# Delta-rule attention and two MoE layers on one core: the first set's preparation emitted as one block, ahead of the weight conversion

## Chip, cores, metric

The kernel runs on one core of a Trainium2 chip. The metric is the device time of one launch in microseconds (us). All times below that begin with a position ("at 61.2") are counted from the first instruction of the profiled execution.

## What is computed

```python
# attention: a state of 48 x 48 per batch and head, updated token by token
k_n = k / (norm(k) + 1e-6)
for t in range(S):                      # S = 768; 4 batches x 8 heads
    y[t] = q[t] @ state
    state += beta[t] * outer(k_n[t], v[t] - k_n[t] @ state)
x = y reshaped to 3072 x 384
# first layer
h = ((x @ w1) * (x @ w2)) @ w3 @ w_out   # w1, w2: 384x1024, w3: 1024x1024, w_out: 1024x384
# second layer
h = h @ w_in; softmax-weighted, normalised per token, scaled by g_ln
out = ln @ w_out2
```

The six weight matrices arrive as 64-bit floats, everything else as 32-bit floats.

## The kernel before

**Attention in chunks.** The 768 tokens of a batch are cut into chunks of 64; heads go in pairs (NP = 4), and six sets of eight chunks (SETC = 8) follow each other. For a set the kernel needs, of every chunk, the Gram matrix of its normalised keys and the product of keys and queries, then the inverse of a small triangular matrix per chunk and head, then a chain of matmuls that carries the state from chunk to chunk. The prologue does this for set 0 before the main loop starts; later sets are prepared inside the main loop, between the matmuls of the first layer.

**Preparation of two chunks**, of which set 0 has four (i = 0 to 3):
- `norm(i)` (L244): square on ScalarE (ACT) at L249, sum on VectorE (DVE) at L250, square root on ACT at L251, add, reciprocal and product on DVE (L252 to L254), then copies of the keys by DMA (tile `kst`).
- `prep_t(i)` (L267): TensorE (PE) transposes the keys (`pk`, L270) and the queries (`pq`, L275) into PSUM; ACT (L272) and DVE (L277) copy them into the one buffer `KQ`, ACT copies parts of the queries into `QA` (L280, L281).
- `prep_g(i)` (L287): 16 matmuls in two PSUM tiles `pg` (L295); ACT copies the Gram parts (L300 to L303) into `GD`, which is a view of the tile `GT`, and into `G21`; DVE masks the key-query part into `QA` (L306).

`KQ` exists once, so the matmuls of one i must end before the copies of the next i start.

**The inverse** (`invert`, L325) works on all of set 0 at once: DVE transposes `GT` into `D1n` (L326), GpSimd (POOL) zeroes `GT`, and 31 pairs of DVE operations (L336, L342) follow, each waiting for the one before. `invert_end` (L346) transposes the result into `Dt` (L347) and `D1n` (L348). The first matmul of the main loop (`pm`, L374) reads `Dt`.

**Weight conversion** is one generator, `wg`. A block of a matrix is loaded by DMA into one of five staging slots (tiles `stage_a`, twice, and `raw_w2s`, three of them). For each half of a block DVE takes the low words (L140), ACT the high words (L143), DVE shifts (L150) and a custom operation adds (L187). The order of the blocks is: four of `w_out`, eight of `w3`, three of `w1`, three of `w2`. A `w3` block is then transposed by PE (`w3p`, L551), copied by ACT (L553) into one of two areas, and multiplied with `w_out` (`wps`, L558): eight products of 384 columns for each of the eight blocks, which sum up in one PSUM tile that exists once. ACT and DVE split the sum (L226, L227) into `Ws`, the product of both matrices; only then is the PSUM tile free for the next block. A slot is loaded again when its block has been converted and, for `w3`, transposed. One `next(wg)` is one small step of this; `conv(x)` takes x steps.

**What sets the order.** A scheduler in the tile framework places the instructions of each engine when the program is built, from the order in which the code emits them and from costs of its own; each engine then runs its list in order. `held[0]` names an instruction behind which the steps of `conv` are kept (`tc.issue_after`), here the last ACT copy of the preparation just emitted. From L787 on the matmuls' order is fixed by hand, up to the end of the main loop.

The prologue's core (L727 to L747):

```python
norm(1)
for i in range(SETC // 2):
    prep_t(i)
    if 0 < i < SETC // 2 - 1:
        norm(i + 1)
    conv(P0)          # P0 = 4
    prep_g(i)
    conv(2 * P0)
held[0] = None
for z, ins in enumerate(invert(0)):
    conv(0.5, ins)
    ...
```

Of the kernel before, what the change touches and what calls it, by code (L numbers as in the profile page):

```python
# [8 lines left out]
F32 = mybir.dt.float32  # L9
# [3 lines left out]
AF = mybir.ActivationFunctionType  # L13
# [7 lines left out]
def kernel(  # L21
# [15 lines left out]
    nc = tc.nc  # L37
# [25 lines left out]
    P0, C0 = 4, 24  # L63
# [10 lines left out]
    const = ctx.enter_context(tc.tile_pool(name="const", bufs=1))  # L74
# [49 lines left out]
    GD = GT.rearrange("p (u j) -> p u j", j=HC)  # L124
# [119 lines left out]
    def norm(i):  # L244
        kt = kt_of(i).rearrange("t p (e x) -> t p e x", e=2)[:, :, :, 0:D]
        sq = small(NP * 2 * D).rearrange("t (p e d) -> t p e d", e=2, d=D)
        ss = pr.tile([128, NP, 2], F32, name="ss")
        rn = pr.tile([128, NP, 2, 1], F32, name="rn")
        nc.scalar.activation(out=sq, in_=kt, func=AF.Square)  # L249
        nc.vector.tensor_reduce(out=ss, in_=sq, axis=AX.X, op=ALU.add)  # L250
        nc.scalar.activation(out=ss, in_=ss, func=AF.Sqrt)  # L251
        nc.vector.tensor_scalar(out=ss, in0=ss, scalar1=1e-6, scalar2=None, op0=ALU.add)  # L252
        nc.vector.reciprocal(out=rn[:, :, :, 0], in_=ss)
        nc.vector.tensor_tensor(out=kt, in0=kt, in1=rn.to_broadcast([128, NP, 2, D]), op=ALU.mult)  # L254
        for cc in range(2):
            sl = (chunk_of(i) + 2 * cc) % RQ
            for h in range(2):
                o = 64 * (1 - h)
                nc.sync.dma_start(
                    out=kst[sl * 2 // RQ][64 * h:64 * h + 64, sl % (RQ // 2)],  # L260
                    in_=kt_of(i)[64 * cc:64 * cc + 64, :, o:o + D],
                )
# [4 lines left out]
    def prep_t(i):  # L267
        pk = ps_prep.tile([128, NP, 128], F32, tag="prep", name="pk")
        for p in range(NP):
            nc.tensor.transpose(pk[:, p, :], kt_of(i)[:, p, :], ident)  # L270
        r = pk.rearrange("r p (c t) -> r c p t", c=2)
        nc.scalar.copy(out=KQ[0:KA, :, :, 0:C], in_=r[0:KA])  # L272
        pq = ps_prep.tile([128, NP, 128], F32, tag="prep", name="pq")
        for p in range(NP):
            nc.tensor.transpose(pq[:, p, :], qt_of(i)[:, p, :], ident)  # L275
        r = pq.rearrange("r p (c t) -> r c p t", c=2)
        (nc.vector.tensor_copy if i < SETC else nc.scalar.copy)(out=KQ[0:KA, :, :, C:128], in_=r[0:KA])  # L277
        sl = chunk_of(i) % RQ
        qa, sl = qa_of(sl)
        nc.scalar.copy(out=qa[0:64, sl:sl + 3:2, :, 1, :], in_=r[0:64])  # L280
        held[0] = nc.scalar.copy(out=qa[64:KA, sl:sl + 3:2, :, 0, :], in_=r[64:KA])  # L281
        if i < 2:
            load(i + 4)
        if i > 3 and i + 2 < NT128:
            load(i + 2)

    def prep_g(i):  # L287
        for cc in range(2):
            c = chunk_of(i) + 2 * cc
            (qa, sl), u0 = qa_of(c % RQ), c % SETC * NP  # L290
            pg = ps_prep.tile([128, NP, 128], F32, tag="prep", name="pg")
            for p in range(NP):
                for h in range(2):
                    r = slice(64 * (1 - h), 64 * (1 - h) + D)
                    nc.tensor.matmul(  # L295
                        pg[64 * h:64 * h + 64, p, :], KQ[r, cc, p, 0:C], KQ[r, cc, p, :],
                        start=True, stop=True, skip_group_check=True,
                    )
            gd = GD[:, u0:u0 + NP, :]
            nc.scalar.copy(out=gd[:, :, :], in_=pg[:, :, 0:HC])  # L300
            nc.scalar.copy(out=G21[:, c % SETC], in_=pg[:, :, 0:HC])
            nc.scalar.copy(out=gd[32:64], in_=pg[32:64, :, HC:C])
            held[0] = nc.scalar.copy(out=gd[96:128], in_=pg[96:128, :, HC:C])  # L303
            for h in range(2):
                r = slice(64 * h, 64 * h + 64)
                nc.vector.tensor_tensor(  # L306
                    out=qa[r, sl, :, h, :], in0=pg[r, :, C:128],
                    in1=mask[r].unsqueeze(1).to_broadcast([64, NP, C]), op=ALU.mult,
                )
# [3 lines left out]
    def load_beta():  # L313
        for b in range(B):
            nc.sync.dma_start(
                out=bd.rearrange("(o k b) p e g i -> o b (p e) k (g i)", k=CPB, b=2)[b // 2, b % 2],
                in_=beta[b].rearrange("h (k x) -> h k x", k=CPB),
            )
        t = bd.rearrange("(n c) p e g i -> e g (c p) n i", c=SETC)
        for h in range(2):  # L320
            for g in range(2):
                r = 64 * h + 32 * g
                nc.sync.dma_start(out=bl[r:r + 32], in_=t[1 - h, g])
# [345 lines left out]
    def weights_first():  # L669
        a = moe.tile([128, 4096], F32, tag="gh", name="stage_a")  # L670

        def slot(tag):
            return lambda: wts.tile([128, 2 * DFF], F32, tag=tag, name="raw_" + tag)

        a0, a1 = (lambda: a[:, 0:2 * DFF]), (lambda: a[:, 2 * DFF:4 * DFF])
        b = [slot(t) for t in ("w2s0", "w2s1", "w2s2")]
        items = list(weights_w([a0, a1] + b))
        items += weights_ab(w1, w1s, "w1s", [b[0], b[1], b[2]])
        items += weights_ab(w2, w2s, "w2s", [
            a0, a1, lambda: moe.tile([128, 2 * DFF], F32, tag="xb", name="raw_xb", bufs=2),  # L680
        ])
        return convert(items, small, queue, 1)

    make_identity(nc, ident)
    wg = weights_first()
    for i in range(4):
# [8 lines left out]
    for h in range(2):  # L695
        nc.gpsimd.affine_select(
            out=mask[64 * h:64 * h + 64], in_=mask[64 * h:64 * h + 64], pattern=[[1, C]],
# [8 lines left out]
    held = [None]  # L706

    def conv(x, ins=None):
        acc[0] += x
        if acc[0] < 1:  # L710
            return
        with (tc.issue_after(ins.ins) if ins is not None and c_done[0] >= CA else tc.issue_after(held[0].ins) if held[0] is not None else nullcontext()):
            while acc[0] >= 1:
                next(wg, None)
                acc[0] -= 1
# [3 lines left out]
    come = nc.gpsimd.tensor_copy(out=seen, in_=qt_of(2)[:, 0, 64:65])  # L719
    with tc.issue_after(come.ins):  # L720
        next(wg)
    nc.gpsimd.memset(GD, 0.0)
    load_beta()
    for c in range(0, RX, 2):
        load_v(c)
# [2 lines left out]
    for i in range(SETC // 2):  # L728
        prep_t(i)
        if 0 < i < SETC // 2 - 1:  # L730
            norm(i + 1)
        conv(P0)
        prep_g(i)
        conv(2 * P0)

    held[0] = None
    for z, ins in enumerate(invert(0)):
# [281 lines left out]
```

## Time and profile before

| | us |
|---|---|
| median of 3 runs (865.22 to 867.65) | 865.59 |
| span of the profiled execution, first to last instruction | 863.0 |
| PE busy (of the span) | 808.5 (94%) |
| DVE busy | 577.3 (67%) |
| ACT busy | 468.3 (54%) |
| POOL busy | 42.4 (5%) |

For the profiled execution no time besides its span is given; the median of the runs is 2.6 us longer than that span, which is what lies around it. "Busy" is the union of an engine's instructions; PE's weight loads are listed apart (PEld). In a timeline a row gives the start, the time taken, the engine, the line of the code, the operation, what is written from what, the count, and in brackets how long the engine had been idle and what ended that. In a window's row the numbers in brackets are counts, and the last three columns are the granted clock of PE as a share of full speed, the busy share of the DMA engines, and GB/s. The granted clock is shown as 1.00 until the first event that the profile holds, so for the first 40 us it is read from durations.

### The profile page before, as it was taken

The numbers are of one execution on the slowest core, as the hardware profiler recorded it, in microseconds if no ns is written. First come the engines' busy times: TensorE is split into PE (matmuls) and PEld (weight loads), VectorE is DVE, ScalarE is ACT, GpSimd is POOL, SyncE is SP. The second block draws the span as 40 slices with busy tenths as digits, with TensorE's granted clock in tenths as the row PEclk, the third lists the DMA queues.
The fourth block names the chain that finished last, engine by engine and source line by source line (L and its number), as shares of the span: only waits on it lengthen the run. The fifth ranks groups of instructions, "written<-read, shape, count | busy, mean of one in ns | idle before, by whom it ended". The sixth has DMA issues, their size and how long they took to land.

```text
span 863.0 us, 22978 instructions
## 1 busy us (share of the span) xinstructions
PE 808.5 (94%) x9488; PEld 738.5 (86%) x9488; DVE 577.3 (67%) x1426; ACT 468.3 (54%) x1127; POOL 42.4 (5%) x94
## 2 busy tenths in 40 slices
PE   4599678999999999999999999999999999999998
PEld 4365466999889999999999999999989999999997
DVE  3889996985497559755975596457656555555553
ACT  4574578457736773576467744566434443443442
POOL 5010000000000000000000000000001000000000
PEclk9999859999999999999999999999999999999999
DMA  9999814041403331333133113043331221221200
GB/s 226 289 235 163 128 20 83 13 93 35 93 26 63 73 75 35 73 70 68 35 65 68 39 38 94 12 135 109 118 125 57 74 64 55 74 65 55 74 28 28
DMA packets 140569, 70.65 MB, mean 82 GB/s; under 512 B 107056, under 2 KB 130864, under 8 KB 138672
## 3 DMA queue, kind: packets, MB, share of 16 engines
q1 hardware_dynamic: 138688, 57.64, 29.3%
q0 software_dynamic: 1776, 11.54, 4.1%
q8 instruction: 75, 1.23, 0.6%
q14 instruction: 30, 0.25, 0.1%
HBM read 47.91 MB, written 14.25 MB: 72 GB/s over the span
## 4 chain that ended last, share of the span: by engine, by line
PE 45%; issue 23%; DVE 16%; ACT 8%; DMA 6%; POOL 2%; SPq 0%; POOLq 0%; ACTq 0%; DVEq 0%
PE pab L585 17%; PE px L609 6%; PE pg L295 4%; DVE tmp L336 3%; PE wps L558 3%; DVE GT L342 2%; PE pu L445 2%; PE pw L419 2%; PE py L488 2%; DMA stage_i<-in_moe_w_in_dram 2%; PE pst L470 1%; PE pm L398 1%; PE ph L909 1%; POOL vr L939 1%; DMA st_o<-in_moe_w_out_dram 1%
## 5 line engine op out<-in xcount | busy, mean ns | idle before, releaser
L585 PE MATMUL pab<-xb,w1s 128*128 128x256 f32 x864 | 123.6, 288 | 5.1 <-DVE asg L593 4.5
L585 PE MATMUL pab<-xb,w2s 128*128 128x256 f32 x864 | 119.2, 283 | 0.0
L585 PEld LDWEIGHTS pab<-xb,w1s 128*128 128x128 f32 x864 | 109.7, 191 | 9.1 <-DVE asg L593 6.1
L609 PE MATMUL px<-gh,Ws 128*128 128x256 f32 x864 | 112.2, 286 | 0.6 <-ACT gh L594 0.5
L585 PEld LDWEIGHTS pab<-xb,w2s 128*128 128x128 f32 x864 | 110.6, 192 | 0.0
L609 PEld LDWEIGHTS px<-gh,Ws 128*128 128x128 f32 x864 | 105.5, 191 | 2.3 <-ACT gh L594 0.7
L962 PE MATMUL po<-w4s,ln 128*128 128x384 f32 x432 | 79.8, 338 | 0.0
L594 ACT CAST gh<-asg 128x256 fp32r<-128x256 f32 x96 | 38.9, 405 | 72.4 <-DVE asg L593 71.6
L909 PE MATMUL ph<-wis,x 128*128 128x512 f32 x288 | 76.7, 401 | 0.0
L962 PEld LDWEIGHTS po<-w4s,ln 128*128 128x128 f32 x432 | 76.1, 188 | 0.0
L925 ACT ACTIVATE e<-ph,nm 128x1024 f32<-128x1024 f32 x24 | 26.8, 1116 | 87.4 <-DVE nm L924 86.0
L593 DVE TENSOR_TENSOR asg<-pab,asg 128x256 f32<-128x256 f32 x96 | 40.4, 421 | 50.4 <-ACT asg L592 50.2
L342 DVE TENSOR_TENSOR GT<-GT,tmp 128x31 f32<-128x31 f32 (+15 forms) x186 | 63.5, 341 | 4.6
L336 DVE TENSOR_TENSOR tmp<-D1n,GT 128x31 f32<-128x31 f32 (+15 forms) x186 | 62.9, 338 | 3.4 <-ACT GT L328 0.2
L306 DVE TENSOR_TENSOR QA<-pg,mask 64x256 f32<-64x256 f32 x96 | 40.5, 422 | 35.6 <-ACT GT L303 29.1
L295 PE MATMUL pg<-KQ 48*64 48x128 f32 x768 | 54.8, 294 | 8.4 <-DVE KQ L277 7.4
L909 PEld LDWEIGHTS ph<-wis,x 128*128 128x128 f32 x288 | 52.4, 189 | 10.5 <-issue 0.2
L592 ACT COPY asg<-pab 128x256 f32<-128x256 f32 x96 | 35.5, 370 | 44.3 <-PE pab L585 41.0
L295 PEld LDWEIGHTS pg<-KQ 48*64 48x64 f32 x768 | 47.4, 147 | 12.3 <-ACT raw_w2s L143 6.0
L924 DVE TENSOR_REDUCE nm<-ph 128x1 f32<-128x1024 f32 x24 | 29.4, 1224 | 40.4 <-PE ph L909 40.4
L926 DVE SCALAR_TENSOR_TENSOR hs<-ph,e 128x1024 f32<-128x1024 f32 x24 | 29.4, 1225 | 30.9 <-ACT e L925 30.9
L595 DVE TENSOR_TENSOR gh<-asg,gh 128x256 fp32r<-128x256 f32 x96 | 40.5, 422 | 13.9 <-ACT gh L594 13.4
(157 smaller groups left out, 1347.8 us busy)
## 6 DMA issues: line engine op xcount, KB each, us to landing
x2d<-xs SPq DMA_DIRECT2D x36, 256.0 KB, 2.3
x<-x2d SPq DMA_DIRECT2D x24, 384.0 KB, 3.7
X<-in_v_dram SPq DMA_DIRECT2D x48, 96.0 KB, 2.9
out_dram<-ot SPq DMA_DIRECT2D x24, 192.0 KB, 1.9
ktok<-in_k_dram SPq DMA_DIRECT2D x22, 192.0 KB, 3.6
qtok<-in_q_dram SPq DMA_DIRECT2D x22, 192.0 KB, 3.6
kst<-ktok SPq DMA_DIRECT2D x88, 48.0 KB, 3.0
raw_w2s<-in_moe_w_dram POOLq DMA_DIRECT2D x4, 1024.0 KB, 8.9
```

The source lines that it names most:

```text
L295: nc.tensor.matmul(pg[64 * h:64 * h + 64, p, :], KQ[r, cc, p, 0:C], KQ[r, cc, p, :], start=True, stop=True, skip_group_check=True,)
L306: nc.vector.tensor_tensor(out=qa[r, sl, :, h, :], in0=pg[r, :, C:128], in1=mask[r].unsqueeze(1).to_broadcast([64, NP, C]), op=ALU.mult,)
L336: yield nc.vector.tensor_tensor(out=t, in0=Lz[:, j, j + 1:HC].unsqueeze(2).to_broadcast([128, m, j + 1]), in1=Tt[:, j, 0:j + 1].unsqueeze( ...
L342: yield nc.vector.tensor_tensor(out=Tt[:, j + 1:HC, 0:j + 1], in0=Tt[:, j + 1:HC, 0:j + 1], in1=t, op=ALU.add)
L585: nc.tensor.matmul(pab[:, e, :], ws[m][:, a, fs], xb[:, b, m, :], start=(n == 0), stop=(n == 3 * NM - 1), skip_group_check=True,)
L592: nc.scalar.copy(out=asb, in_=pab[:, 0, :])
L593: nc.vector.tensor_tensor(out=g, in0=pab[:, 1, :], in1=asb, op=ALU.mult)
L594: nc.scalar.copy(out=gh[:, 0, f, :], in_=g)
L595: gated[0] = nc.vector.tensor_tensor(out=gh[:, 1, f, :], in0=g, in1=gh[:, 0, f, :].bitcast(F32), op=ALU.subtract)
L609: nc.tensor.matmul(px, Ws[:, a, f, js], gh[:, b, f, :], start=(n == 0), stop=(n == 3 * NF - 1),)
L909: nc.tensor.matmul(ph[:, gs], x2[:, m, a, :], wis[m][:, b, gs], start=(n == 0), stop=(n == 3 * NM - 1),)
L962: nc.tensor.matmul(po, ln[:, a, f, :], w4s[f][:, b, :], start=(n == 0), stop=(n == 3 * NF - 1),)
```

## The change

Three edits. A tile of one column is set to 1 and its square root taken on ACT, ahead of everything else, so that the table for square roots is loaded first. The memset of `GD` is dropped; the copies L300, L302 and L303 write all of it. The steps of conversion that stood inside the loop over i (4 and 8 per i, 48 in all) are emitted after it, 48 at once, and are no longer held behind the preparation's copies.

```diff
+    warm = const.tile([128, 1], F32, name="warm")
+    nc.vector.memset(warm, 1.0)
+    nc.scalar.activation(out=warm, in_=warm, func=AF.Sqrt)
     make_identity(nc, ident)
     wg = weights_first()
...
     with tc.issue_after(come.ins):
         next(wg)
-    nc.gpsimd.memset(GD, 0.0)
     load_beta()
...
         prep_t(i)
         if 0 < i < SETC // 2 - 1:
             norm(i + 1)
-        conv(P0)
         prep_g(i)
-        conv(2 * P0)
+    held[0] = None
+    conv(12 * P0)
 
     held[0] = None
     for z, ins in enumerate(invert(0)):
```

How the lists of the engines change, at three places. Lines after L683 are two or three higher in the changed kernel.

**PE, from the preparation of i = 2 on** (`pk`, `pq`, `pg`: preparation; `w3p`, `wps`: the product of `w3` and `w_out`). Before:

```order
L295 MATMUL pg<-KQ 64x128 x7
L551 MATMUL w3p<-ident,raw_w2s_157 128x128 x4
L295 MATMUL pg<-KQ 64x128 x4
L558 MATMUL wps<-area 128x384 x4
L295 MATMUL pg<-KQ 64x128 x5
L551 MATMUL w3p<-ident,raw_w2s_157 128x128 x4
L551 MATMUL w3p<-ident,stage_a 128x128 x4
L270 MATMUL pk<-ident,early 128x128 x4
L275 MATMUL pq<-ident,early 128x128 x4
L558 MATMUL wps<-area 128x384 x4
```

Now:

```order
L295 MATMUL pg<-KQ 64x128 x16
L270 MATMUL pk<-ident,early 128x128 x4
L275 MATMUL pq<-ident,early 128x128 x4
L295 MATMUL pg<-KQ 64x128 x16
L551 MATMUL w3p<-ident,raw_w2s_160 128x128 x7
L558 MATMUL wps<-area 128x384 x4
```

All four preparations now stand ahead of the first `w3p`; before, those of i = 2 and 3 were cut up by the first two blocks of `w3`.

**DVE, at the transpose that starts the inverse** (L326; `Ws` is the split of a finished product, and its number tells which block). Before:

```order
L187 ISA raw_w2s0_331<-raw_w2s0_331,t_531 128x1024
L326 STREAM_TRANSPOSE D1n_97<-GT_104 128x1024
L150 TENSOR_SCALAR raw_w2s1_370<-raw_w2s1_370 128x512
L329 SCALAR_TENSOR_TENSOR D1n_97<-D1n_97,bl_106 128x1024
L187 ISA raw_w2s1_370<-raw_w2s1_370,t_549 128x1024
L187 ISA raw_w2s1_370<-raw_w2s1_370,t_565 128x1024
L227 TENSOR_TENSOR Ws_88<-wps_496,Ws_88 128x384
```

Now:

```order
L187 ISA raw_w2s0_434<-raw_w2s0_434,t_533 128x1024
L326 STREAM_TRANSPOSE D1n_97<-GT_104 128x1024
L227 TENSOR_TENSOR Ws_88<-wps_459,Ws_88 128x384
L329 SCALAR_TENSOR_TENSOR D1n_97<-D1n_97,bl_106 128x1024
L140 TENSOR_SCALAR t_596<-raw_w2s2_481 128x512
```

Before, the splits of blocks 0 and 1 stood ahead of the transpose and that of block 2 (`wps_496`) just behind it; now that of block 0 (`wps_459`) stands behind it, so the inverse is one to two blocks further ahead of the products.

**DVE and PE, where the inverse and the products end.** `wps_722` and `wps_771` are the last two blocks before, `wps_724` and `wps_773` now; a wait on DVE ahead of a product is for the split of the block before it. DVE before, then DVE now:

```order
L336 TENSOR_TENSOR tmp_105<-D1n_97,GT_104 128x31 [waits DVE_49]
L342 TENSOR_TENSOR GT_104<-GT_104,tmp_105 128x31 [waits DVE_49]
L347 STREAM_TRANSPOSE Dt_96<-GT_104 128x32x32 [waits DVE_49]
L227 TENSOR_TENSOR Ws_88<-wps_771,Ws_88 128x384 [waits Activation_49]
L348 STREAM_TRANSPOSE D1n_97<-GT_104 128x32x32
```

```order
L342 TENSOR_TENSOR GT_104<-GT_104,tmp_105 128x31 [waits DVE_49]
L347 STREAM_TRANSPOSE Dt_96<-GT_104 128x32x32 [waits DVE_49]
L348 STREAM_TRANSPOSE D1n_97<-GT_104 128x32x32
L227 TENSOR_TENSOR Ws_88<-wps_724,Ws_88 128x384 [waits Activation_49]
L227 TENSOR_TENSOR Ws_88<-wps_773,Ws_88 128x384 [waits Activation_49]
```

PE now, at the same place:

```order
L558 MATMUL wps_724<-area_117 128x384 [waits DVE_49]
L558 MATMUL wps_724<-area_117 128x384 x3
L558 MATMUL wps_724<-area_118 128x384 x4
L558 MATMUL wps_773<-area_117 128x384 [waits DVE_49]
L558 MATMUL wps_773<-area_117 128x384 x3
L558 MATMUL wps_773<-area_118 128x384 [waits Activation_49]
L558 MATMUL wps_773<-area_118 128x384 x3
L374 MATMUL pm_872<-Dt_96,G21_95 32x32 x16
```

The split of block 6 (`wps_724`) stood nine pairs (L336, L342) ahead of the inverse's end before (as `wps_722`); now it stands behind both transposes of the result, and block 7's product waits for it, with the main loop's first matmul (`pm`) behind that product. From there on all lists are the same in both kernels.

## Rows read from the trace of the kernel before

**Rows 1.** A window of 10 us in the inverse: busy PE, PEld, DVE, ACT, POOL, clock, DMA.

```profile
80.00:90.00 10.00, 9.71 (x39) 6.01 (x38) 9.47 (x26) 3.76 (x8) 0.49 (x1) 1.00 1.10 173
```

**Rows 2.** PE's groups from 39 to 100 us: count, busy us, mean ns, idle.

```profile
L558 PE MATMUL wps<-area 128*128 128x384 f32 x128 | 44.5, 499 | 2.9 <-DVE Ws L227 1.8 <-ACT area L553 1.2
L295 PE MATMUL pg<-KQ 48*64 48x128 f32 x44 | 3.7, 283 | 0.0
```

**Rows 3.** Timeline of the first normalisation.

```profile
4.51 0.55 DVE L250 TENSOR_REDUCE ss<-t 128x8 f32<-128x384 f32 x1 [4.51 <-ACT t L249]
...
7.27 1.28 ACT L251 ACT_TABLE_LOAD   x1
8.56 0.21 ACT L251 ACTIVATE ss<-ss 128x8 f32<-128x8 f32 x1
...
9.25 0.56 DVE L254 TENSOR_TENSOR ktok<-ktok,rn 128x384 f32<-128x384 f32 x1
```

**Rows 4.** Timeline: first Gram matmuls, then those of the next round (i = 1).

```profile
12.83 3.68 PE L295 MATMUL pg<-KQ 48*64 48x128 f32 x32 [0.94 <-DVE KQ L277]
...
19.28 3.68 PE L295 MATMUL pg<-KQ 48*64 48x128 f32 x32 [0.88 <-DVE KQ L277]
```

**Rows 5.** Timeline: DVE's conversion steps: a short pair, and a long one.

```profile
32.35 0.42 DVE L140 TENSOR_SCALAR t<-raw_w2s 128x512 uint32<-128x512 uint32 x1
...
32.68 0.35 DVE L150 TENSOR_SCALAR raw_w2s<-raw_w2s 128x384 uint32<-128x384 uint32 x1
...
66.74 0.69 DVE L187 CUSTOM_DVE_ANT_0 stage_a<-stage_a,t 128x1024 uint16<-128x1024 uint16 x1
...
67.34 0.21 DVE L342 TENSOR_TENSOR GT<-GT,tmp 128x31 f32<-128x31 f32 x1
```

**Rows 6.** Timeline: first products, last Gram copy, start of the inverse.

```profile
39.00 3.63 PE L558 MATMUL wps<-area 128*128 128x384 f32 x8
...
58.71 0.26 ACT L303 COPY GT<-pg 32x128 f32<-32x128 f32 x1
...
61.20 1.95 DVE L326 STREAM_TRANSPOSE D1n<-GT 128x1024 f32<-128x1024 f32 x1
```

**Rows 7.** Timeline: the inverse ends, the last product, the first merge.

```profile
93.49 0.55 DVE L227 TENSOR_TENSOR Ws<-wps,Ws 128x384 fp32r<-128x384 f32 x1
...
94.09 5.43 PE L558 MATMUL wps<-area 128*128 128x384 f32 x16 [1.59 <-DVE Ws L227]
...
99.56 0.48 ACT L226 CAST Ws<-wps 128x384 fp32r<-128x384 f32 x1 [6.16 <-PE wps L558]
...
100.25 1.91 DVE L347 STREAM_TRANSPOSE Dt<-GT 128x1024 f32<-128x1024 f32 x1
...
102.19 2.06 ACT L387 COPY TW<-Dt 32x256 f32<-32x256 f32 x5 [2.16 <-DVE Dt L347]
...
102.47 1.99 DVE L348 STREAM_TRANSPOSE D1n<-GT 128x1024 f32<-128x1024 f32 x1
...
104.95 0.26 PE L398 MATMUL pm<-xp,D1n 32*32 32x32 f32 x2 [1.67 <-ACT xp L382]
```

**Rows 8.** Timeline after it: ACT's cast of w1, then the merge's next copy.

```profile
106.56 0.62 ACT L226 CAST w1s<-raw_w2s 128x512 fp32r<-128x512 f32 x1 [0.30 <-DVE raw_w2s L187]
...
107.20 0.37 ACT L402 ACTIVATE TW<-pm 32x256 f32<-32x256 f32 x1
```

**Rows 9.** Gram matmuls at either clock, and the window of the first.

```profile
110.00:120.00 10.00, 7.98 (x100) 6.99 (x100) 8.65 (x18) 8.75 (x21) 0.00 (x0) 0.50 0.01 2
114.20 3.68 PE L295 MATMUL pg<-KQ 48*64 48x128 f32 x32
...
129.69 2.14 PE L295 MATMUL pg<-KQ 48*64 48x128 f32 x32
```

**Rows 10.** DMA issues, 0 to 130 us: KB each, median us to landing.

```profile
raw_w2s<-in_moe_w_dram POOLq DMA_DIRECT2D x4, 1024.0 KB, 8.9
stage_a<-in_moe_w_dram POOLq DMA_DIRECT2D x4, 1024.0 KB, 5.8
```

## The prediction, made before the changed kernel ran

> **What bounds the kernel now.** The totals say only that PE is busy for 94% of the span and DVE for 67%. The change touches the first 105 us, so I read that stretch: windows for the busy engine, the groups of PE, then the timeline for who waits for whom. In the window of 80 to 90 us both PE (9.71 of 10) and DVE (9.47) are full [rows 1]. PE's groups tell what fills it: the products `wps` take 44.5 us of the 61 between 39 and 100, the Gram matmuls left over from the preparation 3.7, and the longest idle time ahead of the products, 2.9, is a wait for a split on DVE [rows 2]. The timeline then shows two chains that end together. DVE runs the inverse: its first transpose starts at 61.20 [rows 6], its last pair of transposes at 100.25 and 102.47 [rows 7]. PE runs the last product from 94.09 for 5.43 us [rows 7]. The first merge needs both, and its first matmul that reads `D1n` stands at 104.95 [rows 7]. From there on the lists are the same in both kernels, on engines that are rarely free, so I let a shift of that point pass to the end one for one.
>
> **The start.** ACT loads the table for 1.28 us between the second square and the first square root, which comes at 8.56, though DVE's sum was ready at 4.51 + 0.55 = 5.06 [rows 3]. With the table loaded while the first data is still on its way, the root can stand at 5.1: 8.56 - 5.06 = 3.5 earlier. The path behind it is the Gram matmuls at 12.83 [rows 4]; the second normalisation now has its DVE product (0.56 [rows 3]) in front of the copies, so I take 3.0 of the 3.5: first Gram at 9.8.
>
> **The memset.** It runs on POOL, which is busy for 5% of the span, and no instruction of the window's other engines is released by it; I cost it at nothing. What covers it is that POOL has only loads to issue beside it, and those stand ahead of it in its list.
>
> **The preparation in one block.** A round lasts from one burst of Gram matmuls to the next, 19.28 - 12.83 = 6.45, the burst itself 3.68 [rows 4]. I add 0.9 once, for the masks and the third normalisation that stand in front of DVE's copy of `pq` (an estimate from the 0.56 of such a product [rows 3]). The fourth burst ends at 9.8 + 3 x 6.45 + 0.9 + 3.68 = 33.7; four copies of some 0.26 to 0.5 and two masks later, at about 35.7, `GT` is complete. Before, its last copy stood at 58.71 [rows 6]. So the inverse could start 23 us earlier. It won't, since DVE's list has conversions ahead of it.
>
> **What DVE has to do first.** The spacing of two instructions in the timeline prices them: a short step 32.68 - 32.35 = 0.33, a long add 67.34 - 66.74 = 0.60 [rows 5]; for the add of 768 columns I take 0.75 of it, 0.45. Between the last masks and L326 the new list has 8 long adds (4.80), 3 of 768 (1.35) and 20 short steps (6.60): 12.75, to 48.4. Two waits come on top. The fifth `w3` block's ACT step stands behind a copy that waits for the first products; I allow 1.2, less than a half of the 3.63 that a half product takes at first [rows 6]. And the fourth and fifth blocks must have been loaded. Their slots come free at about 36.2 and 38.4 and DVE wants them at 43.5 and 46.0, 7.3 and 7.6 later; loads of this kind took 8.9 in the median, those into the other slots 5.8 [rows 10]. So they are 0 to 1.6 late, and I take half, 0.8. L326 then starts at 50.4 where it was 61.20: 10.8 earlier.
>
> **The inverse gets longer.** It took 100.25 - 61.20 = 39.05 with DVE full [rows 1], so what is added within it adds to it. By the two lists that is 3 more L140, 3 more L150, 2 more long adds and one more split at 0.47 (100.25 to 102.47 is 2.22, the transpose alone about 1.76 [rows 7]): 0.99 + 0.99 + 1.20 + 0.47 = 3.65. It ends at 50.4 + 42.7 = 93.1, against 100.25: of 10.8 us gained 7.1 are left.
>
> **The new wait.** Block 7's product waits for the split of block 6. That split stood well ahead of the inverse's end, with its product 0.60 behind it (93.49 to 94.09 [rows 7]); now it stands behind both transposes. 93.1 + 1.76 + 1.99 + 0.60 = 97.4, and with 5.43 for the product 102.9. Queued behind it on PE is the merge's `pm`, which before could start when `Dt` was done at 100.25 + 1.91 = 102.16. Here ACT's cast of the product (0.48) comes first, then the same copies as between 102.16 and 104.95, 2.79 [rows 7]: the first matmul with `D1n` at about 106.15, 1.2 later than before. On DVE the conversions follow the last split, 102.9 + 0.48 + 0.55 = 103.9, where they followed the transpose that ended at 102.47 + 1.99 = 104.46 [rows 7], 0.5 earlier. That counts too, because ACT's cast at 106.56 waits for DVE and the merge's next copy, 107.20, stands behind it [rows 8]. Between 0.5 earlier and 1.2 later I take 0.4 later.
>
> A check from PE's side: from 39.00 to 99.52 it took 60.5 [rows 6, 7]. Without 3.7 of Gram matmuls [rows 2] and a little over 1 of transposes that now stand ahead (an estimate), it needs 55.6. DVE's first steps after the masks, 3 adds of 768, 6 short steps and a long add, are 3.93; with about 1.9 for the first transposes and their copy the products start at 35.7 + 5.8 = 41.5. PE alone would then be done at 97.1, nearly 6 us before 102.9. What ends last is DVE's inverse, then the product behind it.
>
> **The queues.** POOL's order of loads stays, each issued when its slot is free, and so most of the early ones later; that is the 0 to 1.6 above. On SP one thing moves: four copies of keys of the fifth normalisation stand ahead of the first loads for `w1`. These are wanted only in the second half of the inverse, so I cost that at nothing; if they came late, DVE's L140 would wait there, with the inverse behind it.
>
> **Sum.** The profiled execution has a span of 863.0, and the median of the runs, 865.6, is 2.6 longer, which I take as unchanged. 865.6 + 0.4 = **866.0**, no change: a measurement of this kernel can tell about 0.3%, 2.6 us.
>
> **Rival, faster: the bursts run at the upper clock.** [...] With four preparations in a row PE works more closely than before. If the later three ran at the upper level, two rounds and the last burst would give up 1.5 each, some 4.6, of which ACT's copies would take back about 1: 3.5 earlier, 862.5. It speaks against this that in 110 to 120 us PE was busy for 7.98 of 10 with such work and the clock stayed at 0.50 [rows 9], and that the bursts now at 12.83 and 19.28 both took 3.68 [rows 4]. [...] Chance 0.18.
>
> **Rival, slower: the loads come late.** The blocks' slots are freed later than before, because the conversions that free them stand behind the masks. The place is DVE's L140 of the fourth to seventh `w3` block, the price the landing behind the time at which DVE gets there, and it decides from about 7.5 us per load. At the 8.9 that the loads took [rows 10] the first pair is 0.8 later than I allowed, and two later ones, each wanted some 7.4 after its slot is free, 1.5 each: 866.0 + 0.8 + 3.0 = 869.8. For it speaks that 8.9 is the median, against it that the other slots took 5.8. Chance 0.28.
>
> **Chances.** The forecast has 0.54; of it 0.05 lies more than 2.6 below 865.6 and 0.07 above. Of the faster rival 0.15 and of the slower one 0.23 lie outside. So faster 0.20, within 0.3% 0.50, slower 0.30. The range takes in both rivals' times with 0.7 to 1.0 beyond: 861.5 to 870.5.
>
> **What would show it.** Right: the first root near 5.1 and the first Gram near 9.8; bursts of 3.68; L326 near 50 and L347 near 93; the last product near 97, released by DVE's split, and the first matmul with `D1n` near 106. The faster rival: bursts of 2.14 before 35 us, L326 near 47. The slower one: L140 idle on a DMA of `raw_w2s` or `stage_a` between 40 and 60. Wrong altogether: the inverse's 39 us becoming shorter instead of longer, `pm` released by something other than the last product, or stages behind 107 us that differ although their lists don't.

## The result, and the profile after

The changed kernel takes 874.4 us (median of 12 runs, 866.05 to 877.85) against 866.35 (12 runs, 865.01 to 867.65): a ratio of 1.0079, 95% interval 1.0055 to 1.0103 (ratios here and below are taken over all the runs; the quotient of these two medians is 1.0093). It is slower by 0.8%, where no change was forecast (866.0), and it lies outside the range of 861.5 to 870.5. The profiled execution has a span of 873.0, 10.0 longer than before. Its time is 874.83, 1.8 more than its span, and the other runs on record have 1.7 to 1.8 as well: of the 2.6 between median and span before, the rest would then be the difference between executions.

The timeline of the changed kernel, at the start and at the first and the last burst of Gram matmuls (columns as in [rows 3, 4]; here and below lines after L683 are two or three higher):

```profile
5.40 0.21 ACT L251 ACTIVATE ss<-ss 128x8 f32<-128x8 f32 x1 [0.62 <-DVE ss L250]
...
10.43 3.68 PE L295 MATMUL pg<-KQ 48*64 48x128 f32 x32 [0.87 <-DVE KQ L277]
...
29.78 3.68 PE L295 MATMUL pg<-KQ 48*64 48x128 f32 x32 [0.88 <-DVE KQ L277]
...
34.21 0.26 ACT L303 COPY GT<-pg 32x128 f32<-32x128 f32 x1
```

The root stands at 5.40 instead of 8.56, the last Gram copy at 34.21 instead of 58.71 [rows 3, 6]. So far the change does what it says. The inverse then starts, and soon stands still (same view):

```profile
49.45 1.92 DVE L326 STREAM_TRANSPOSE D1n<-GT 128x1024 f32<-128x1024 f32 x1
...
56.78 0.18 DVE L336 TENSOR_TENSOR tmp<-D1n,GT 128x31 f32<-128x31 f32 x1
...
62.94 0.43 DVE L140 TENSOR_SCALAR t<-stage_a 128x512 uint32<-128x512 uint32 x1 [5.98 <-DMA stage_a<-in_moe_w_dram]
63.28 0.20 DVE L342 TENSOR_TENSOR GT<-GT,tmp 128x31 f32<-128x31 f32 x1
...
65.06 8.40 PE L558 MATMUL wps<-area 128*128 128x384 f32 x16 [6.02 <-DVE Ws L227]
```

L326 is 11.75 earlier than at 61.20 [rows 6]. Behind the first L336, a conversion of the seventh `w3` block waits 5.98 for its load, with the L342 of the same pair queued behind it. The split of a finished product is queued there too, so PE stands for 6.02, and the next product takes 8.40 where the same 16 matmuls took 5.43 in [rows 7]. The windows show what goes with it (columns as in [rows 1]: PE, PEld, DVE, ACT, POOL, granted clock, DMA share, GB/s):

```profile
50.00:60.00 10.00, 7.07 (x27) 4.18 (x27) 6.73 (x12) 3.68 (x8) 1.99 (x3) 1.00 1.07 225
60.00:70.00 10.00, 4.94 (x8) 2.82 (x9) 7.06 (x25) 1.45 (x3) 0.00 (x0) 0.54 0.40 142
```

From 60 to 70 us the granted clock is 0.54, where it was 1.00 from 50 to 60; in steps of 2 us it is 1.00 from 58 to 60, 0.72 from 60 to 62, 0.50 from 62 to 70, 0.72 from 70 to 72 and 1.00 from 72 to 80. The issues of DMA between 49.3 and 51.2 us, with the KB of each and the time to landing, and two rows of the queues' timelines, show what the load was up against:

```profile
stage_a<-in_moe_w_dram POOLq DMA_DIRECT2D x1, 1024.0 KB, 12.9
raw_xb<-in_moe_w_dram SPq DMA_DIRECT2D x2, 384.0 KB, 9.3
raw_xb<-in_moe_w_dram SPq DMA_DIRECT2D x1, 128.0 KB, 12.1
```

```profile
49.47 1.54 SPq L178 DMA_DIRECT2D raw_xb<-in_moe_w_dram  x3
...
49.98 0.53 POOL L178 DMA_DIRECT2D stage_a<-in_moe_w_dram  x1 [3.40 <-PE w3p L551]
```

`raw_xb` is the last block of `w2`, which no conversion reads before 127.2. Its place in memory is free from the start, so its transfers go out as soon as SP's queue reaches them: at 49.47, behind a key copy issued from 48.84 for 0.59. Before, they went out at 54.6 to 56.6; in the same view of the kernel before, the seventh `w3` block's load, issued at 49.64, had landed after 6.2:

```profile
stage_a<-in_moe_w_dram POOLq DMA_DIRECT2D x1, 1024.0 KB, 6.2
```

The end of the inverse, in the timeline of the changed kernel, to be laid beside [rows 7]:

```profile
100.19 1.92 DVE L347 STREAM_TRANSPOSE Dt<-GT 128x1024 f32<-128x1024 f32 x1
...
103.77 0.50 DVE L227 TENSOR_TENSOR Ws<-wps,Ws 128x384 fp32r<-128x384 f32 x1
104.33 7.12 PE L558 MATMUL wps<-area 128*128 128x384 f32 x16 [3.78 <-DVE Ws L227]
111.38 0.69 PE L374 MATMUL pm<-Dt,G 32*32 32x32 f32 x32
...
114.60 0.60 PE L398 MATMUL pm<-xp,D1n 32*32 32x32 f32 x26 [2.53 <-ACT xp L382]
```

L347 starts where it did before, 100.19 against 100.25: all of the earlier start is gone. The last product then stands behind the transposes, as the lists said, and again behind idle time (3.78), so that it takes 7.12. The first merge's matmul with `D1n` comes at 114.60 instead of 104.95, 9.65 later.

### The profile page after: what moved, and what is told of

It reads as the page before. It is cut to its first block, busy times and chain, and to the rows that moved or that the text cites. A ratio compares the mean times of both kernels' runs of the same rounds, so it can differ in the third digit from the quotient of the medians.

```text
span 873.0 us, 22981 instructions
## 1 busy us (share of the span) xinstructions
PE 816.0 (93%) x9488; PEld 743.6 (85%) x9488; DVE 576.1 (66%) x1427; ACT 467.3 (54%) x1127; POOL 41.8 (5%) x93
## 4 chain that ended last, share of the span: by engine, by line
PE 46%; issue 23%; DVE 18%; ACT 6%; DMA 5%; POOL 2%; SPq 0%; POOLq 0%; DVEq 0%; ACTq 0%
PE pab L585 16%; PE px L609 7%; PE pg L295 5%; DVE tmp L336 4%; DVE GT L342 3%; PE pw L419 2%; PE pu L445 2%; PE wps L558 2%; PE py L488 2%; PE pst L470 2%; DMA stage_a<-in_moe_w_dram 1%; PE pm L398 1%; PE ph L911 1%; POOL vr L941 1%; DMA st_o<-in_moe_w_out_dram 1%
## 5 line engine op out<-in xcount | busy, mean ns | idle before, releaser
L593 DVE TENSOR_TENSOR asg<-pab,asg 128x256 f32<-128x256 f32 x96 | 40.4, 420 | 50.4 <-ACT asg L592 50.3
L342 DVE TENSOR_TENSOR GT<-GT,tmp 128x31 f32<-128x31 f32 (+15 forms) x186 | 63.4, 341 | 4.6
L336 DVE TENSOR_TENSOR tmp<-D1n,GT 128x31 f32<-128x31 f32 (+15 forms) x186 | 62.8, 338 | 3.3 <-ACT GT L328 0.2
L558 PE MATMUL wps<-area 128*128 128x384 f32 x128 | 49.1, 541 | 11.4 <-DVE Ws L227 11.1
L295 PEld LDWEIGHTS pg<-KQ 48*64 48x64 f32 x768 | 49.5, 152 | 6.9 <-issue 2.5
L558 PEld LDWEIGHTS wps<-area 128*128 128x128 f32 x128 | 26.4, 212 | 30.5 <-DVE Ws L227 12.2
```

The source lines that it names most:

```text
L295: nc.tensor.matmul(pg[64 * h:64 * h + 64, p, :], KQ[r, cc, p, 0:C], KQ[r, cc, p, :], start=True, stop=True, skip_group_check=True,)
L336: yield nc.vector.tensor_tensor(out=t, in0=Lz[:, j, j + 1:HC].unsqueeze(2).to_broadcast([128, m, j + 1]), in1=Tt[:, j, 0:j + 1].unsqueeze( ...
L342: yield nc.vector.tensor_tensor(out=Tt[:, j + 1:HC, 0:j + 1], in0=Tt[:, j + 1:HC, 0:j + 1], in1=t, op=ALU.add)
L558: nc.tensor.matmul(acc[m], w3t[:, j, :], wos[kk // (NF // 2)][:, kk % (NF // 2), :], start=(kk == 0), stop=(kk == NF - 1),)
L593: nc.vector.tensor_tensor(out=g, in0=pab[:, 1, :], in1=asb, op=ALU.mult)
```

## The experiments

**Theory L**: the moved conversions and preparations let two transfers meet (the last `w2` block's and the seventh `w3` block's), and the removal of the memset changed the order in which DVE splits the products (this part was added after run 4); both make DVE and PE stand still (PE for 6.02 and 3.78 in the changed kernel) and PE's granted clock fall (0.54 from 60 to 70 us, 0.83 from 100 to 110). **Rivals**: S, the early start alone does the harm; Q, only the last product behind the inverse matters; D, the load is slow by itself. All ratios are to runs of the kernel before on the same chip. The comparisons of traces rest on the merge's first matmul with `D1n`, called **M** below: 104.95 before, 114.60 in the changed kernel.

**1. The early root alone**, in the kernel before:

```diff
+    warm = const.tile([128, 1], F32, name="warm")
+    nc.vector.memset(warm, 1.0)
+    nc.scalar.activation(out=warm, in_=warm, func=AF.Sqrt)
     make_identity(nc, ident)
```

> The kernel before with the early square root alone; the lists of the other engines are those of before. Theory L (what was lost comes from the moved conversions: the load of w3's seventh block lands behind the last w2 block's transfers, DVE and PE stand still for 6 us and PE's clock falls): the root costs nothing, its 3 us may reach the merge in part, 0 to 3 us faster than before, 863 to 866. Rival S (the start itself is what hurts: earlier Gram matmuls move the transfers of keys and of weights into each other): as slow as the changed kernel, 872 to 876.

865.0 against 865.8, ratio 0.9993 (0.9982 to 1.0005). M stands at 104.24. The start is harmless, and S falls; of some 2 us at the first Gram matmuls 0.7 reach the merge:

```profile
10.85 3.68 PE L295 MATMUL pg<-KQ 48*64 48x128 f32 x32 [1.29 <-DVE KQ L277]
...
104.24 0.91 PE L398 MATMUL pm<-xp,D1n 32*32 32x32 f32 x26 [2.04 <-ACT xp L382]
```

**2. The last `w2` block loaded late**, in the changed kernel: its pieces on each queue are issued behind those of the block before it (item 17 of the list of blocks is the last).

```diff
+        last = {}
...
-                    (queue(i, src) if queue else nc.sync).dma_start(out=d, in_=src)
+                    eng = queue(i, src) if queue else nc.sync
+                    key = eng is nc.sync
+                    with tc.issue_after(last[key].ins) if queue and i == 17 else nullcontext():
+                        got = eng.dma_start(out=d, in_=src)
+                    if i < 17:
+                        last[key] = got
```

> The changed kernel with the loads of the last w2 block issued behind those of the block before it, instead of before the w1 blocks. [...] Rival Q (the loss is the last product queued behind the inverse, wherever that ends): no change, 873 to 876. Rival D (the load is slow by itself, at any neighbour): the wait stays at 4 to 6, 872 to 876.

868.4 against 865.8, ratio 1.0014 (0.9996 to 1.0032), 0.4 above theory L's 865 to 868 for this run (with it went a wait of L140 for that load of under 1 instead of 5.98, 42 to 44 from L326 to L347, and M at 105 to 107). The load lands after 5.4 instead of 12.9, the granted clock in the 60 to 70 us window is 1.00 instead of 0.54, and the inverse runs from 48.59 to 91.21, 42.62 against 50.74 in the changed kernel. No L140 waits more than 0.23 for a load. In the trace these numbers of theory L hold (M is 105.63); Q and D fall. The edit also moves the fourth piece of the block, 128 KB on POOL's queue; in the changed kernel that was issued at 39.22 and had landed after 8.5, before the slow load was issued. The key copies ahead of the `w2` transfers on SP are not moved (39.48 to 49.76 here, 38.42 to 49.42 in the changed kernel), so they are not what made the load slow. What stays is the second half: the product behind the inverse still takes 7.12 after 3.50 of idle time. The profile (DMA issues, window, timeline; lines are six higher than in the changed kernel):

```profile
stage_a<-in_moe_w_dram POOLq DMA_DIRECT2D x1, 1024.0 KB, 5.4
```

```profile
60.00:70.00 10.00, 9.46 (x39) 6.03 (x38) 9.53 (x27) 3.78 (x7) 0.51 (x1) 1.00 0.81 186
```

```profile
48.59 1.95 DVE L332 STREAM_TRANSPOSE D1n<-GT 128x1024 f32<-128x1024 f32 x1
...
91.21 1.93 DVE L353 STREAM_TRANSPOSE Dt<-GT 128x1024 f32<-128x1024 f32 x1
...
95.36 7.12 PE L564 MATMUL wps<-area 128*128 128x384 f32 x16 [3.50 <-DVE Ws L233]
...
105.63 0.60 PE L404 MATMUL pm<-xp,D1n 32*32 32x32 f32 x26 [2.53 <-ACT xp L388]
```

**3. The split of block 6 ahead of the transposes**, in the changed kernel; `done` keeps the splits' instructions (the lines that fill it are left out).

```diff
     held[0] = None
-    invert_end(0)
+    with tc.issue_after(done[6].ins):
+        invert_end(0)
```

> The changed kernel with one instruction moved: DVE's split of block 6 stands ahead of both transposes that end the inverse. The wait for the load stays. Theory L with the new wait as its second half: block 6's product ended at 100.6, so the last product can start near 101.7 instead of 104.3 and, with less idle time ahead of it, take 5.4 instead of 7.1: the merge 3 to 4.5 earlier, 870 to 872. Rival (the split only takes its time from the transposes, the merge waits for these): no change, 873 to 876.

868.1 against 865.8, ratio 1.0019 (0.9996 to 1.0042): more is gained than the expected 870 to 872. In the profiled run the load is late again (a wait of 4.11), and it takes 11.6. The last product starts at 99.32, together with the transposes, and takes 5.43 (timeline):

```profile
61.82 0.43 DVE L140 TENSOR_SCALAR t<-stage_a 128x512 uint32<-128x512 uint32 x1 [4.11 <-DMA stage_a<-in_moe_w_dram]
...
99.18 1.94 DVE L347 STREAM_TRANSPOSE Dt<-GT 128x1024 f32<-128x1024 f32 x1
99.32 5.43 PE L560 MATMUL wps<-area 128*128 128x384 f32 x16 [1.16 <-DVE Ws L227]
...
107.90 0.60 PE L398 MATMUL pm<-xp,D1n 32*32 32x32 f32 x26 [2.53 <-ACT xp L382]
```

From the last product's start to M it takes 8.58, against 10.27 in the changed kernel, and that start is 0.14 behind L347 instead of 4.14. These two, 1.7 and 4.0, are the price of the new wait; 1.0 more of the 6.7 is L347 itself, where the wait for the load was shorter.

**4. Both edits.**

> Both of the above. Theory L: the inverse ends near 92, the last product is no longer behind it and ends by 98 to 100, the merge's matmul with D1n at 100 to 103: 861 to 864, faster than before. Rival Q: as the kernel with the split first alone. Rival D: 869 to 872.

863.5 against 865.8, ratio 0.9964 (0.9948 to 0.998): faster than the kernel before, as expected. M stands at 102.30, 2.65 earlier than before. The two causes together are the whole loss: M is 8.97 earlier than in the changed kernel with the first edit, 6.70 with the second, 12.30 with both. Q would have left this run where the third was. The last product and M (timeline):

```profile
93.72 5.43 PE L566 MATMUL wps<-area 128*128 128x384 f32 x16 [1.05 <-DVE Ws L233]
...
102.30 0.71 PE L404 MATMUL pm<-xp,D1n 32*32 32x32 f32 x26 [2.53 <-ACT xp L388]
```

**5. The memset kept** (the changed kernel with `nc.gpsimd.memset(GD, 0.0)` back in its place):

> The changed kernel with the memset of GD kept: the early root and the block of preparations alone. The scheduler then orders DVE in another way: the split of block 6 stands one step ahead of the inverse's last pair instead of behind both transposes, and of the conversions fewer stand ahead of the inverse's first pair. Theory L, second half (part of the loss is the last product behind the inverse, and the memset's removal brought it): no idle time of 3.8 ahead of the last product, which takes 5.4, and the load of the seventh w3 block may still be late by 0 to 6; 863 to 870. Rival (the memset is as free as it looks from POOL's side): 873 to 876.

864.8 against 866.45, ratio 0.9983 (0.9957 to 1.0009). The lists change far from POOL: without any edit on it the split of block 6 stands one step ahead of the inverse's last pair, and the last product starts ahead of the transposes, with 1.13 of idle time in front. ACT's list shows how far the change reaches: the first Gram copy stands at 24.75, behind the conversions, though the memset had ended at 14.92; in the changed kernel it stands at 12.44, ahead of them. Timelines of the changed kernel, then of this run (M is 104.25):

```profile
12.44 0.27 ACT L300 COPY GT<-pg 128x128 f32<-128x128 f32 x1 [0.41 <-PE pg L295]
```

```profile
13.95 0.97 POOL L725 MEMSET GT<- 128x1024 f32 x1
...
24.75 0.27 ACT L300 COPY GT<-pg 128x128 f32<-128x128 f32 x1
...
63.80 0.43 DVE L140 TENSOR_SCALAR t<-stage_a 128x512 uint32<-128x512 uint32 x1 [3.23 <-DMA stage_a<-in_moe_w_dram]
...
95.67 5.43 PE L558 MATMUL wps<-area 128*128 128x384 f32 x16 [1.13 <-DVE Ws L227]
96.48 1.95 DVE L347 STREAM_TRANSPOSE Dt<-GT 128x1024 f32<-128x1024 f32 x1
```

The wait for a load is still there, 3.23, now for the block after, which took 9.5. The single runs go from 860.3 to 873.3, four of the twelve below 862 and four above 868.5.

**6. Late `w2` loads in the kernel before**, the edit of the second run:

> The kernel before with the loads of the last w2 block issued late, as in the run of the changed kernel with that edit. Theory L: before, these transfers start 5 us after the load that they delay in the changed kernel, and no L140 waits for it, so nothing is gained: 864 to 867, the same as before. Rival (these transfers are in the way in any order, and the gain has nothing to do with the change): 1 to 4 faster, 861 to 864.5.

866.4 against 866.45, ratio 0.9998 (0.9981 to 1.0015). Nothing, as theory L says: the edit is worth something only where the change put the transfers in the way.

**7. A second PSUM tile for the sum**, with late `w2` loads, in the changed kernel:

```diff
-                    acc[m] = ps_px.tile([128, DM], F32, tag="x2", name="wps")
+                    acc[m] = (ps_prep.tile([128, DM], F32, tag="prep", name="wps") if m % 2
+                              else ps_px.tile([128, DM], F32, tag="x2", name="wps"))
```

> The changed kernel with the late w2 loads and a second PSUM tile for the sum of the products, taken in turns, so that a block's product no longer waits for the split of the block ahead of it. Theory L: the wait for a split goes (some 1.1 per block), the last product doesn't stand behind the inverse, the inverse (DVE) ends near 91 to 93 and bounds the merge: matmul with D1n at 97 to 100, 858 to 862. Rival (PE has nothing to gain there, ACT's copies and DVE's conversions set its pace): as the kernel with both edits, 862 to 865.

864.8 against 866.45, ratio 0.9991 (0.9972 to 1.0009): a miss, and inside the rival's 862 to 865. The inverse does end earlier, at 89.04, but the last half product starts at 98.53: its operand's copy stands on ACT behind copies of the next set's preparation, which the scheduler has put there. M is 106.15. The wait for a split was replaced by one for ACT, as the rival has it (timeline):

```profile
89.04 1.97 DVE L353 STREAM_TRANSPOSE Dt<-GT 128x1024 f32<-128x1024 f32 x1
...
97.89 0.59 ACT L559 COPY area<-w3p 128x512 f32<-128x512 f32 x1
...
98.53 4.46 PE L565 MATMUL wps<-area 128*128 128x384 f32 x8 [2.83 <-ACT area L559]
```

**8. The memset kept and the `w2` loads late**, the edits of runs 5 and 2 together:

> The changed kernel with the memset kept and the w2 loads late: the two halves of the loss taken away without touching the order by hand. Theory L: as the kernel with both edits, 861 to 864.5, faster than before. Rival: between the kernel before and the changed one, 866 to 872.

860.5 against 866.45, ratio 0.9941 (0.9918 to 0.9963), six runs from 859.9 to 863.2, the median 0.5 below the expected 861 to 864.5: the fastest of all, 0.6% under the kernel before, and without the scatter of run 5. The inverse runs from 48.97 to 90.80, the last product lies beside its last step, M is 99.08 (timeline), 5.87 earlier than before:

```profile
48.97 1.94 DVE L332 STREAM_TRANSPOSE D1n<-GT 128x1024 f32<-128x1024 f32 x1
...
90.49 5.43 PE L564 MATMUL wps<-area 128*128 128x384 f32 x16 [1.21 <-DVE Ws L233]
...
90.80 1.96 DVE L353 STREAM_TRANSPOSE Dt<-GT 128x1024 f32<-128x1024 f32 x1
...
99.08 0.60 PE L404 MATMUL pm<-xp,D1n 32*32 32x32 f32 x26 [2.54 <-ACT xp L388]
```

## Why the prediction was wrong

**The sum, term by term**, from the profile of the changed kernel:

| step | forecast | measured | difference |
|---|---|---|---|
| L326 starts | 50.4 | 49.45 | -0.95 |
| L326 to L347 | 42.7 | 50.74 | +8.04 |
| L347 to the last product's start | 4.35 | 4.14 | -0.21 |
| the last product, to `pm` | 5.43 | 7.05 | +1.62 |
| `pm` to M | 3.25 | 3.22 | -0.03 |
| M | 106.15 | 114.60 | +8.45 |

**Right.** The root, the bursts, the chain of conversions ahead of L326 and the steps behind the inverse, except the last product's own time, came within 1 us each. The bursts kept 3.68 (at 10.43 and at 29.78), so the faster rival didn't happen; its 1.5 per burst is an estimate, 3.68 less the 2.14 of [rows 9], and that four preparations in a row would run like the latter was a guess that no run shows. That the inverse gets 3.65 longer was right as well: with the load out of the way it takes 42.62 (run 2), where 42.7 was forecast. M is 105.63 there where 106.15 was, but that is partly luck: L326 starts 1.8 earlier than forecast, and the last product takes 1.7 longer. That the product behind the inverse is the last link was right too, and run 3 shows its price.

**Wrong: the queues.** "On SP one thing moves" was read from the order of SP's list, and the order is what stayed. What moved is the time. The `w2` transfers stand behind the key copies of the third and fourth normalisation; these are ready earlier, so the transfers went out at 49.47, half a microsecond ahead of a load that DVE gets to at 56.96. That load doesn't move (49.98, and 49.64 before), because PE's transposes free its slot (its issue follows `w3p` in both). The prediction counted as moved what had changed its place in a list, and put at nothing what goes out earlier on a queue that runs ahead; it cost the 5.98 of the wait, and run 2, which takes it away, has M 8.97 earlier.

**Wrong: the size of a late load.** The slower rival had the mechanism and the place (L140 of the fourth to seventh block), but took 8.9, the slower of two medians [rows 10], for its upper end. The load took 12.9. With 7.4 free it was 5.5 late by that reckoning, and L140 waited 5.98, where the rival allowed 1.5. A median over four loads that met different traffic is no bound for one that meets more.

**Wrong: what an idle PE costs.** Both waits were priced as waits alone. After 6.02 of idle time a product took 8.40 instead of 5.43, after 3.78 another took 7.12: 3.0 and 1.7 more. In run 2 it took 7.12 again after 3.50; after 1.05 to 1.59, in the kernel before and in runs 3, 4, 5 and 8, it took 5.43. The granted clock was 0.54 in the window of the first and 0.83 in that of the second (the changed kernel; columns as in [rows 1]):

```profile
100.00:110.00 10.00, 6.22 (x15) 3.10 (x14) 4.24 (x4) 0.97 (x2) 0.00 (x0) 0.83 1.04 138
```

In steps of 2 us the granted clock there was 1.00 from 102 to 104, 0.81 from 104 to 106, 0.50 from 106 to 108, 0.84 from 108 to 110 and 1.00 from 110 to 112. So each of the two idle stretches has a fall to 0.50 within it or behind it; with the load out of the way (run 2) PE was busy for 9.46 of the 10 from 60 to 70 us and the granted clock was 1.00. What sets the clock beyond this is not shown. The slow product also kept DVE waiting inside the inverse: beside the 5.98 for the load there are waits of 1.16 for ACT's cast and of 1.20 for a conversion that stood behind that product, 8.34 in all against the 8.04 in the table.

**Wrong: the memset at nothing.** As work it is nothing. But its absence let the scheduler place the Gram copies differently (the first at 12.44 instead of 24.75, run 5), and DVE's list with them; run 5, which differs from the changed kernel by that line alone, has no product that waits behind the inverse. I had read the resulting lists and not asked which of the three edits made them.

**Smaller points.** The 0.4 in the sum, taken between 0.5 earlier and 1.2 later at the merge, has no run behind it: in the changed kernel M is 9.65 later and the span 10.0 longer. And the 2.9 of [rows 2] is all the idle time ahead of the products together, 1.8 of it for the split; the prediction read it as one wait, but no term rests on it.

What was not tried is the reverse, to push these transfers in front of that load in the kernel before. The changed kernel's own runs go down to 866.05; the load may have come in time in those, but no trace shows it.

## What to carry to other kernels

When work is emitted earlier, follow not only the instructions that change places but every transfer whose queue is freed earlier: here prefetches first read at 127.2 ran ahead until, from 49.47 on, they met a load that was needed (12.9 instead of 6.2), and in run 6 it cost nothing that the runs can tell (ratio 0.9998) to issue them behind the loads that are. Price a new wait on PE with the clock that follows it: here 3.0 more behind 6.02 of idle time, 1.7 behind 3.78. And where a scheduler orders the program, build each edit alone and compare the lists, since the cheapest one may be what moves them.

## What was not expected of the hardware

The seventh block's load, 1 MB, took 5.2 to 6.2 where the `w2` transfers went out later than it (before and in runs 2 and 4), and 12.9 and 11.6 (the changed kernel and run 3) when these three, 0.9 MB in all, were issued from another queue within 1.4 us of it. In the changed kernel its landing at 62.9 is the last of the four. It was not simply queued behind the others: from 53.5 to 60.5 both queues moved data, POOL's (q0) 0.89 MB and SP's (q1) 0.52, but at 204 GB/s together. From 52.5 to 55 in run 2 POOL's queue moved 0.93 MB nearly alone, at 378 GB/s. Why the total falls is not shown. The DMA view of these two stretches:

```profile
DMA packets 216, 1.43 MB, mean 204 GB/s; under 512 B 43, under 2 KB 43, under 8 KB 43
q0 software_dynamic: 109, 0.89, 65.8%
q1 hardware_dynamic: 106, 0.52, 32.7%
```

```profile
DMA packets 138, 0.94 MB, mean 378 GB/s; under 512 B 24, under 2 KB 24, under 8 KB 24
q0 software_dynamic: 122, 0.93, 89.3%
```

The shift at the merge passes on nearly one for one for a long way and is then blurred. The matmuls `py` at 580.63 before come 9.1 later in the changed kernel (589.69), 2.4 later in run 3 (583.02) and 3.2 earlier in run 4 (577.42), where M is 9.65 later, 2.95 later and 2.65 earlier. In run 2 M is 0.7 later than before and these `py` are 0.1 later (580.70), but the span is 4.4 longer; part of that is one stretch late in the run, in which PE idles for 1.21 and the granted clock is 0.91. Idle time alone does not settle it: in run 3 PE idles for 1.17 at the same place, and the clock stays at 1.00. Single spans are thus no measure of an edit here, and the verdicts above rest on the medians and ratios. The windows of run 2, then of the kernel before:

```profile
620.00:640.00 20.00, 18.64 (x135) 17.86 (x134) 12.98 (x34) 8.41 (x21) 0.00 (x0) 0.91 0.32 100
```

```profile
620.00:640.00 20.00, 19.40 (x142) 18.24 (x141) 11.99 (x32) 8.58 (x20) 0.00 (x0) 1.00 0.37 119
```
